# Gate and value products of a gated layer: eight block products per two-by-two block become Strassen's seven, in three chunks of 768 tokens

## The chip, the cores and the metric

The kernel runs on one core of one Trainium2 chip. The core has five engines with their own instruction streams, each worked off in order: PE (TensorE, matrix products into the eight PSUM banks), DVE (VectorE), ACT (ScalarE), POOL (GpSimd) and SP (SyncE, which here issues every DMA transfer). The metric is the time of one execution on the device, in microseconds (us). Lower is better.

## The reference

Three stages follow each other: attention with a decaying causal mask (4 batches, 8 heads, 576 positions, head size 64), a bilinear layer, and a gated layer with an RMS norm ahead of it. Cut to what matters:

```python
x = attention(q, k, v, f)                 # 2304 tokens x 512
x = ((x @ w1) * (x @ w2)) @ w3 @ w_out    # 512 -> 1024 -> 1024 -> 512
xn = x / sqrt(mean(x * x) + 1e-6) * g
gate, val = xn @ w_gate, xn @ w_val       # both 512 -> 1536
out = (silu(gate) * val) @ w_out2         # 1536 -> 512
```

## The kernel before

All data are 32-bit floats. PE multiplies them in its reduced format fp32r, and to keep the precision each operand is split into a high part (the value cast to fp32r) and a low part (the rest). One exact product is then three matmuls: high by high, high by low, low by high.

Nothing is issued in the order of the source. Every piece of work is entered in a planner (class `Plan`) with the engines that may do it, its assumed length, the names that it reads and writes and, for PE, a due time. `Plan.order` then writes out one static order for all engines. Work with two or three possible engines (`copy`, `sub`) goes to the one that would end it first.

The program has two parts in time. The first holds attention, the bilinear layer and the norm (lines up to 691); the normed tokens go to the DRAM tensor `yn_d`, transposed, 288 tokens at a time. The second is the gated layer, which the change rewrites:

- Tokens are taken in five chunks: four of 512 and one of 256. `load_x` fetches a chunk of `yn_d` and splits it into `xnh` and `xnl`, with two buffers, so that a chunk is ready long before it is needed.
- Over the 1536 hidden columns run 12 blocks `fb` of 128. For a block, `gv` makes two PSUM groups, gate and value, of 12 matmuls each (four pieces of the contraction by three passes, L762). They use two of the banks 0 to 3, and the next block uses the other two. ACT then takes the silu of the gate (L768), DVE multiplies it by the value (L769), ACT casts the result to `zh` (L770), and DVE subtracts for `zl` (L771).
- `wout` of the block before follows on PE: for each tile of 128 tokens three matmuls of 512 columns (L793) add into one of four accumulators (`wide`, banks 4 and 5). After the last block each accumulator is copied to one of two buffers `o` (L801 on DVE, L803 on ACT) and stored (L806).
- The weights come as 64-bit-wide data, 1 MB per block. `unit` loads a block into one of two buffers `raw`, converts it in place (Prelu on ACT, L553, and two integer operations on DVE, L554 and L555) and splits it into high and low tiles (L243 to L245, L236). In this kernel all 18 blocks of the second part are converted once, at 480 to 602 us, and stay in SBUF.

Of the kernel before, what the change touches and what calls it, by code (L numbers as in the profile page):

```python
# [13 lines left out]
F32 = mybir.dt.float32  # L14
# [8 lines left out]
P = 128  # L23
# [6 lines left out]
KF2 = DF2 // P  # L30
CH = S // 2
NEG = -1.0e30
FROWS = D + 4
# [5 lines left out]
PRE = 3  # L39
# [32 lines left out]
class Plan:  # L72
# [36 lines left out]
    def begins(self):  # L109

        ops = self.ops
        last = max(o[3] for o in ops if o[3] is not None) + 20000
        by = [last] * len(ops)
        for i in range(len(ops) - 1, -1, -1):
            alts, _, deps, at = ops[i]
            e, ns, _ = alts[0]
            t = by[i] - ns - self.LAG[e]
            if e == "SP":
                t -= 2250
            if at is not None and e == "PE":  # L120
# [81 lines left out]
def body(ctx, tc, q, k, v, f, w12, w3, wo1, wgv, wo2, g, out):  # L202
# [46 lines left out]
    def dma(nbytes, fn, r=(), w=(), at=0):  # L249
        plan.op([("SP", nbytes / (250 if nbytes < 2e5 else 420), False)], lambda e: fn(), r, w)  # L250
# [9 lines left out]
    cn_d = dram.tile([NH, 4, S], F32, name="cn_d")  # L260

# [6 lines left out]
    wpool = ctx.enter_context(tc.tile_pool(name="wpool", bufs=1))  # L268
    m1 = left.enter_context(tc.tile_pool(name="m1", bufs=1))
# [268 lines left out]
    def unit(raw, key, src, h_l, outkey, at, at_load, r_load=(), w_load=(), r_out=(), over=None, parts=1):  # L538

        r_out = list(r_out)  # L540
# [9 lines left out]

        act(1024, lambda: A.activation(f32(hi()), f32(hi()), AF.Prelu, scale=2.0**-112, alpha=2.0**32), [key], [kh], at, 210)  # L553
        dve(1024, lambda: V.tensor_scalar(out=lo(), in0=lo(), scalar1=2.0**-29, scalar2=7.0, op0=ALU.mult, op1=ALU.min), [key], [kl], at, rate=0.52, lock=True)  # L554
        dve(1024, lambda: V.scalar_tensor_tensor(out=lo(), in0=hi(), scalar=3, in1=lo(), op0=ALU.logical_shift_left, op1=ALU.bitwise_or), [key, kh], [kl], at, lock=True)  # L555
        n = 1024 // parts
        for c in range(parts):
            cs = slice(c * n, (c + 1) * n)
            ko = outkey + (c,) if outkey == ("w3",) else outkey
            wh, wl = ([ko + (m,)] + ([over + (m,)] if over else []) for m in "hl")  # L560
            copy(n, lambda cs=cs: h_l()[0][:, cs], lambda cs=cs: f32(lo()[:, cs]), [key, kl] + r_out, wh)
            sub(n, lambda cs=cs: h_l()[1][:, cs], lambda cs=cs: f32(lo()[:, cs]), lambda cs=cs: f32(h_l()[0][:, cs]), [key, kl, ko + ("h",)], wl)

    w12t = [[get(("W", i, m), wpool, [P, 1024], F32R, tag=f"W{i}{m}", name=f"W{i}{m}") for m in "hl"] for i in range(KF)]
    wo1t = [[get(("wo", i, m), wpool, [P, 1024], F32R, tag=f"W{4 + i}{m}", name=f"wo{i}{m}") for m in "hl"] for i in range(4)]
# [128 lines left out]
    chunks = [(c, min(512, NT - c)) for c in range(0, NT, 512)]  # L694
# [8 lines left out]
    w2units = []  # L703
    for fb in range(KF2):
        w2units.append(("wg", fb))
        if fb % 2 == 0:
            w2units.append(("wo2", fb // 2))
    w2t = {}
    for i, (kind, n) in enumerate(w2units):
        for m in "hl":  # L710
            tag = f"W{i - PRE}{m}" if PRE <= i < PRE + KF else f"{kind}{m}{n}"
            where_ = rpool if i < PRE else wpool if i < PRE + KF else lpool
            w2t.setdefault((kind, n), []).append(get((kind, n, m), where_, [P, 1024], F32R, tag=tag, name=f"{kind}{m}{n}"))
    raw2 = [get(("raw2", i), rpool, [P, 2048], F32, name=f"raw2{i}") for i in range(2)]
    xn2 = [[get(("xn", p, m), lpool if p else rpool, [P, KD, 512], F32R, name=f"xn{m}{p}") for m in "hl"] for p in range(2)]
    s_ = get("s", rpool, [P, 512], F32, name="s")
    z_t = [[get(("z", p, m), rpool, [P, 512], F32R, name=f"z{m}{p}") for m in "hl"] for p in range(2)]
    o_t = [get(("o", i), lpool, [P, DM], F32, name=f"o{i}") for i in range(2)]
    raw2n = [0]

    def w2_unit(i, at):
        kind, n = w2units[i]
        p = raw2n[0] % 2
        raw2n[0] += 1
        unit(raw2[p], ("raw2", p), (wgv if kind == "wg" else wo2)[n], lambda: tuple(t() for t in w2t[kind, n]), (kind, n), at, at,
             ["right"], (), ["left"] if i >= PRE + KF else (), ("W", i - PRE) if PRE <= i < PRE + KF else None)

# [3 lines left out]
    def load_x(ci, at):  # L731
        c, n = chunks[ci]
        p, rp = ci % 2, raw2n[0] % 2
        raw2n[0] += 1
        key = ("raw2", rp)

        def r():
            return raw2[rp]().rearrange("p (k n) -> p k n", k=KD)[:, :, 0:n]

        dma(2048.0 * n, lambda: SP.dma_start(out=r(), in_=yn_d[:, :, c:c + n]), yn_keys(c, n) + ["right"], [key, key + ("lo",), key + ("hi",)], at)  # L740
        for t in range(2):
            ks = slice(2 * t, 2 * t + 2)
            extra = ["left"] if p else []
            act(2 * n, lambda ks=ks: A.copy(xn2[p][0]()[:, ks, 0:n], r()[:, ks]), [key] + extra, [("xnh", p, t)], at)
            dve(2 * n, lambda ks=ks: V.tensor_sub(xn2[p][1]()[:, ks, 0:n], r()[:, ks], f32(xn2[p][0]()[:, ks, 0:n])),
                [key, ("xnh", p, t)] + extra, [("xnl", p, t)], at, lock=True)

    gvn = [0]

    def gv(ci, fb):  # L750
        n, p = chunks[ci][1], ci % 2
        gvn[0] += 1
        zp = gvn[0] % 2
        b_ = [2 * zp, 2 * zp + 1]
        t = [bank[i][:, 0:n] for i in b_]
        for m in range(2):
            def run(m=m):
                wh, wl = (w2t["wg", fb][i]().rearrange("p (m k i) -> p m k i", m=2, k=KD) for i in range(2))
                xh_, xl_ = (xn2[p][i]() for i in range(2))
                for kt in range(KD):  # L760
                    for i, (a, x) in enumerate(((wh, xh_), (wh, xl_), (wl, xh_))):
                        T.matmul(t[m], a[:, m, kt, :], x[:, kt, 0:n], start=(kt == 0 and i == 0), stop=(kt == KD - 1 and i == 2))  # L762
            pe(n, run, [("wg", fb, "h"), ("wg", fb, "l"), "right"] + [(a, p, i) for a in ("xnh", "xnl") for i in range(2)],
               [("bank", b_[m])], clock[0], 12)
            tick(12 * (2 + 0.4475 * n))
        at = clock[0]
        zh, zl = z_t[zp]
        act(n, lambda: A.activation(s_()[:, 0:n], t[0], AF.Silu), [("bank", b_[0]), "right"], ["s"], at)  # L768
        dve(n, lambda: V.tensor_mul(s_()[:, 0:n], t[1], s_()[:, 0:n]), [("bank", b_[1])], ["s"], at)  # L769
# [120 lines left out]
    for n, (kind, i) in enumerate(units):  # L890
# [4 lines left out]
        if (kind, i) == ("wo", 3):  # L895
            wc_group(0, WC0, WCP)
# [104 lines left out]
```

## Time and profile before

| | |
|---|---|
| time of the kernel, median of three runs (lowest, highest) | 1012.09 us (1010.34, 1013.09) |
| span of the profiled execution, first to last instruction | 1007.6 us |
| what lies around the span, from the median | 4.5 us |
| PE busy | 990.0 us, 98% of the span |
| DVE, ACT, POOL busy | 57%, 45%, 15% |
| chain of work that ended last | PE 88%, DVE 6%, ACT 2%, DMA 2% |
| first product of the gated layer on PE | 552.31 us |

Of the profiled execution only the span is recorded, no device time of its own; the last line but three is the difference of the median and this span. A busy PE says little by itself, because the recorded matmuls overlap: the end of each lies some 165 ns behind the start of the next. What a matmul costs in a dense stream is read from the distance of their starts, which the chain's pieces give (so many matmuls in so many us).

### The profile page before, as it was taken

Reading aid. Unit: us, or ns where it says so; the run is one execution under the profiler, and the core shown is the slowest. Engines: PE = TensorE matmul, PEld = TensorE weight load, DVE = VectorE, ACT = ScalarE, POOL = GpSimd, SP = SyncE. Lnnn points to the kernel's source line nnn. Section 1 sums busy time; section 2 is a strip of 40 time slices with the busy share of each in tenths; the row PEclk is TensorE's granted clock in tenths of the full one; section 3 lists DMA queues with packets and bytes.
Section 4 is the critical chain, followed back from the end, with each engine's and each line's share of the span. In section 5 each row is a group of like instructions: output and inputs, shape, how many; then the busy total and the mean of one; then the engine's idle time right before and its main releaser. Section 6 shows DMA issues by size and latency. Waiting matters only on the chain.

```text
span 1007.6 us, 15378 instructions
## 1 busy us (share of the span) xinstructions
PE 990.0 (98%) x5880; PEld 880.3 (87%) x5880; DVE 573.8 (57%) x1232; ACT 458.0 (45%) x1012; POOL 153.2 (15%) x197
## 2 busy tenths in 40 slices
PE   7899999999999999999999999999999999999997
PEld 4687889999999999999999888888888888888896
DVE  7899998787878778692959881221122111211121
ACT  6888786666765667563543431211122112111121
POOL 3165233213221231302022100000000000000000
PEclk9999999999999999999999999999999999999999
DMA  8853542121121211002435542010001000100010
GB/s 261 244 196 133 211 141 67 38 62 46 50 61 45 68 51 57 26 25 84 150 126 192 190 168 83 22 42 1 1 1 43 0 1 1 42 1 1 11 32 22
DMA packets 28002, 75.42 MB, mean 75 GB/s; under 512 B 3612, under 2 KB 12316, under 8 KB 23000
## 3 DMA queue, kind: packets, MB, share of 16 engines
q1 hardware_dynamic: 27928, 74.44, 22.5%
q8 instruction: 46, 0.75, 0.3%
q14 instruction: 28, 0.23, 0.1%
HBM read 64.38 MB, written 10.03 MB: 74 GB/s over the span
## 4 chain that ended last, share of the span: by engine, by line
PE 88%; DVE 6%; ACT 2%; DMA 2%; issue 1%; SPq 0%; ACTq 0%; DVEq 0%
PE bank L762 30%; PE bank L638 20%; PE bank L661 10%; PE wide L793 8%; PE bank L793 7%; PE bank L468 4%; PE wide L508 4%; PE bank L394 1%; PE bank L395 1%; DVE PTl L475 1%; DMA tmp<-in_f 1%; PE wide L395 1%; PE wide L394 1%; DMA rk<-x 1%; PE wide L514 1%
## 5 line engine op out<-in xcount | busy, mean ns | idle before, releaser
L769 DVE TENSOR_TENSOR s<-bank,s 128x512 f32<-128x512 f32 (+1 forms) x60 | 38.3, 638 | 275.9 <-PE bank L762 275.9
L762 PE MATMUL bank<-xnl,wgh 128*128 128x512 f32 (+1 forms) x480 | 177.8, 370 | 0.0
L762 PE MATMUL bank<-xnh,wgh 128*128 128x512 f32 (+1 forms) x480 | 177.8, 370 | 0.0
L762 PE MATMUL bank<-xnh,wgl 128*128 128x512 f32 (+1 forms) x480 | 177.4, 369 | 0.0
L768 ACT ACTIVATE s<-bank 128x512 f32<-128x512 f32 (+1 forms) x60 | 33.3, 555 | 191.8 <-PE bank L762 190.4
L762 PEld LDWEIGHTS bank<-xnh,wgh 128*128 128x128 f32 x480 | 90.3, 188 | 16.9
L762 PEld LDWEIGHTS bank<-xnl,wgh 128*128 128x128 f32 x480 | 90.4, 188 | 16.3
L762 PEld LDWEIGHTS bank<-xnh,wgl 128*128 128x128 f32 x480 | 90.3, 188 | 16.0
L770 ACT CAST zh<-s 128x512 fp32r<-128x512 f32 (+1 forms) x60 | 34.7, 578 | 131.7 <-DVE s L769 131.7
L475 DVE TENSOR_TENSOR PTl<-bank,PTh 128x512 fp32r<-128x512 f32 (+3 forms) x116 | 65.2, 585 | 27.5 <-ACT PTh L474 27.3
L661 PE MATMUL bank<-uh,Wch 128*128 128x288 f32 x256 | 77.1, 301 | 0.0
L661 PE MATMUL bank<-ul,Wch 128*128 128x288 f32 x256 | 75.7, 296 | 0.0
L661 PE MATMUL bank<-uh,Wcl 128*128 128x288 f32 x256 | 75.5, 295 | 0.0
L474 ACT CAST PTh<-bank 128x512 fp32r<-128x512 f32 (+3 forms) x116 | 54.5, 505 | 26.4 <-PE bank L468 21.7
L771 DVE TENSOR_TENSOR zl<-s,zh 128x512 fp32r<-128x512 f32 (+1 forms) x60 | 38.3, 638 | 34.4 <-ACT zh L770 34.4
L661 PEld LDWEIGHTS bank<-ul,Wch 128*128 128x128 f32 x256 | 48.2, 188 | 0.1
L661 PEld LDWEIGHTS bank<-uh,Wcl 128*128 128x128 f32 x256 | 48.2, 188 | 0.0
L661 PEld LDWEIGHTS bank<-uh,Wch 128*128 128x128 f32 x256 | 48.2, 188 | 0.0
L793 PE MATMUL wide<-wo2h,zh 128*128 128x512 f32 x120 | 47.5, 396 | 0.7 <-ACT o L803 0.7
L793 PE MATMUL wide<-wo2h,zl 128*128 128x512 f32 x120 | 47.5, 396 | 0.0
L793 PE MATMUL wide<-wo2l,zh 128*128 128x512 f32 x120 | 47.4, 395 | 0.0
L508 PE MATMUL wide<-PTl,V 128*128 128x512 f32 (+4 forms) x145 | 44.1, 324 | 0.9 <-DVE PTl L475 0.9
(350 smaller groups left out, 2538.9 us busy)
## 6 DMA issues: line engine op xcount, KB each, us to landing
raw<-in_wgv SPq DMA_DIRECT2D x12, 1024.0 KB
rk<-in_k SPq DMA_DIRECT2D x62, 144.0 KB
raw<-in_wo SPq DMA_DIRECT2D x6, 1024.0 KB
rv<-in_v SPq DMA_DIRECT2D x32, 160.0 KB
nrm<-in_w SPq DMA_DIRECT2D x5, 1024.0 KB
rq<-in_q SPq DMA_DIRECT2D x32, 144.0 KB
yn_d<-nrm SPq DMA_DIRECT2D x8, 576.0 KB
raw<-yn_d SPq DMA_DIRECT2D x4, 1024.0 KB
```

What stands on the lines that cost most here:

```text
L468: T.transpose(o[:, c * P:(c + 1) * P], PB[p][i][:, kb * P:(kb + 1) * P], ident)
L474: act(n, lambda: A.copy(PTh[:, pt:pt + n], o[:, lo:lo + n]), [], [("PTh", pt), key], at, 55)
L475: dve(n, lambda: V.tensor_sub(PTl[:, pt:pt + n], o[:, lo:lo + n], f32(PTh[:, pt:pt + n])), [("PTh", pt)], [("PTl", pt), key], at)
L508: pe(w, lambda s_=s_, o=o, w=w, c=c, kb=kb, m=m, src=src: T.matmul(t[:, o:o + w], V2[p][:, kb, :], src[:, c:c + w], start=(s_ == 0 and m = ...
L638: T.matmul(o, a, x[:, kt, :], start=(kt == 0 and i == 0), stop=(kt == KD - 1 and i == 2))
L661: T.matmul(o, a[:, es], x[:, ft, :], start=(ft == 0 and i == 0), stop=(ft == KF - 1 and i == 2))
L762: T.matmul(t[m], a[:, m, kt, :], x[:, kt, 0:n], start=(kt == 0 and i == 0), stop=(kt == KD - 1 and i == 2))
L768: act(n, lambda: A.activation(s_()[:, 0:n], t[0], AF.Silu), [("bank", b_[0]), "right"], ["s"], at)
L769: dve(n, lambda: V.tensor_mul(s_()[:, 0:n], t[1], s_()[:, 0:n]), [("bank", b_[1])], ["s"], at)
L770: act(n, lambda: A.copy(zh()[:, 0:n], s_()[:, 0:n]), ["s"], [("zh", zp)], at)
L771: dve(n, lambda: V.tensor_sub(zl()[:, 0:n], s_()[:, 0:n], f32(zh()[:, 0:n])), ["s", ("zh", zp)], [("zl", zp)], at, lock=True)
L793: T.matmul(acc2[t], a[:, ts_], w, start=(fb == 0 and i == 0), stop=(fb == KF2 - 1 and i == 2))
```

## The change

The two-by-two block structure is: the two halves of the contraction (256 each) by the gate and the value columns of a block, and for the tokens two halves of 384. Eight block products give gate and value for both halves of the tokens; the changed kernel forms them from seven products, by Strassen's method in Winograd's form.

- **Operands of the tokens.** `load_x` loads 768 tokens, forms four sums or differences of 128 x 768 and splits seven operands `xop` (there is one set, rewritten at each of the two changes of chunk).
- **Operands of the weights.** `widen` converts a raw block as before, puts four combinations of 128 x 256 into the free halves of the buffer and stores all of it in a DRAM tensor, `sw_d` (for the output weights `wo_d`, without combinations). For six gate and value blocks and three output blocks this is done during the first part (`todo`), for the others when chunk 0 first needs them. `load_w` loads a block for each of the 36 units (three chunks by 12 blocks) and splits it into one of three buffers `swt`, seven operands wide; in the second and third chunk the load is from `sw_d`. The six tiles of output weights still stay in SBUF.
- **A unit.** `gate(u)` makes seven products of six matmuls with 384 columns (L843), in two banks alone, 0 and 1, in turn. Three products start a bank anew and four add onto what stands there; between them ACT copies a bank out (`c1`, `c2`, `c5`) or takes the silu, and DVE adds (`c1`, `c5`, `c2`). The six `wout` tiles of the units before stand between the products. The accumulators of `wout` are now six: `wide` and banks 2 to 5.

The core of the diff (of the removed code only the products):

```diff
-        for m in range(2):
-            def run(m=m):
-                wh, wl = (w2t["wg", fb][i]().rearrange("p (m k i) -> p m k i", m=2, k=KD) for i in range(2))
-                xh_, xl_ = (xn2[p][i]() for i in range(2))
-                for kt in range(KD):
-                    for i, (a, x) in enumerate(((wh, xh_), (wh, xl_), (wl, xh_))):
-                        T.matmul(t[m], a[:, m, kt, :], x[:, kt, 0:n], start=(kt == 0 and i == 0), stop=(kt == KD - 1 and i == 2))
...
+NOP, TH = 7, 384
+TC = 2 * TH
...
+    def widen(kind, i, raw, key, w_load=(), r_load=(), at=None):
...
+            combine(256, t(0), b(3), b(0), keys[:2], [kh, tk[0]])
+            combine(256, t(2), b(2), b(3), keys, [tk[2]])
+            combine(256, t(1), b(2), t(0), keys + [tk[0]], [tk[1]])
+            combine(256, t(3), b(1), t(1), keys + [tk[1]], [tk[3]])
+            keys += tk
+        dma(1.05e6, lambda: SP.dma_start(out=(sw_d if kind == "wg" else wo_d)[i], in_=raw()), keys, [("wd", kind, i)], due=at)
...
+        for n, (c, e, src) in enumerate(((0, 768, lambda: lo()[:, 0:768]), (768, 1792, hi))):
+            split(e - c, lambda c=c, e=e: w()[:, c:e], lambda c=c, e=e: w()[:, SW // 2 + c:SW // 2 + e], src, keys + ["wfree" if b < 2 else "left"], ("sw", b, n, "h"), ("sw", b, n, "l"))
...
+            for kt in range(2):
+                for i, (a, c) in enumerate(((0, 0), (0, 1), (1, 0))):
+                    T.matmul(o, w[:, a, j, kt], x[c][:, kt], start=start and kt == 0 and i == 0, stop=kt == 1 and i == 2, skip_group_check=not start)
...
+        product(u, 0, 0, al, True)
+        act(TH, lambda: A.copy(c1(), pa), [ka] + free, ["c1"])
+        wout(u - 2, 4)
+        product(u, 1, 1, be, True)
+        dve(TH, lambda: V.tensor_add(c1(), c1(), pb), [kb], ["c1"])
+        act(TH, lambda: A.activation(s1(), c1(), AF.Silu), ["c1"] + free, [("s", 0)])
+        wout(u - 2, 5)
+        product(u, 4, 4, al, False)
+        act(TH, lambda: A.copy(c2(), pa), [ka] + free, ["c2"])
+        wout(u - 1, 0)
+        product(u, 3, 3, be, True)
+        act(TH, lambda: A.copy(c5(), pb), [kb] + free, ["c5"])
+        wout(u - 1, 1)
+        product(u, 5, 5, al, False)
+        dve(TH, lambda: V.tensor_add(c5(), c5(), pa), [ka], ["c5"])
+        wout(u - 1, 2)
+        product(u, 2, 6, be, False)
+        dve(TH, lambda: V.tensor_add(c2(), c2(), pb), [kb], ["c2"])
+        mix(s1, s1, c2, ["c2"], [("s", 0)])
+        z_out(u % 2, 0, s1)
+        wout(u - 1, 3)
+        product(u, 6, 2, al, False)
+        act(TH, lambda: A.activation(s2(), pa, AF.Silu), [ka] + free, [("s", 1)])
+        mix(s2, s2, c5, ["c5"], [("s", 1)])
+        z_out(u % 2, 1, s2)
```

How the static order moves is shown at three places. The first is PE in the steady state. Before, this is the end of one value group (bank_60 is bank 1) and the start of the output products behind it; `wgh`, `wgl` are the weights' parts, `xnh`, `xnl` those of the tokens:

```order
L762 MATMUL bank_60<-xnh_6281,wgh_6284 128x512
L762 MATMUL bank_60<-xnl_6288,wgh_6284 128x512
L762 MATMUL bank_60<-xnh_6281,wgl_6285 128x512
L793 MATMUL wide<-wo2h_6208,zh_6000 128x512
L793 MATMUL wide<-wo2h_6208,zl_6010 128x512
L793 MATMUL wide<-wo2l_6209,zh_6000 128x512
```

After, this is one whole unit of the last chunk; bank_59 and bank_60 are banks 0 and 1, the weights lie in `lbig` or `wbig`, L869 are the output products (bank_61 to bank_64 and `wide` are their accumulators):

```order
L843 MATMUL bank_59<-xop,lbig 128x384 x6
L869 MATMUL bank_64<-lbig,wbig 128x512 x3
L843 MATMUL bank_60<-xop,lbig 128x384 x6
L843 MATMUL bank_59<-xop,lbig 128x384 x6
L869 MATMUL wide<-lbig,wbig 128x512 x6
L843 MATMUL bank_60<-xop,lbig 128x384 x6
L843 MATMUL bank_59<-xop,lbig 128x384 x6
L869 MATMUL bank_61<-lbig,wbig 128x512 x3
L843 MATMUL bank_60<-xop,lbig 128x384 x6
L869 MATMUL bank_62<-lbig,wbig 128x512 x3
L843 MATMUL bank_59<-xop,lbig 128x384 x6
L869 MATMUL bank_63<-lbig,wbig 128x512 x3
```

A bank that was left alone for a whole block is now used again after two or three rows.

The second place is DVE in the middle of a chunk. Before (here around a change of chunk, with the split of a new chunk's tokens, L745):

```order
L769 TENSOR_TENSOR s<-bank_60,s 128x512
L745 TENSOR_TENSOR xnl_5215<-raw_5152,xnh_5198 128x1024 x2
L771 TENSOR_TENSOR zl_6063<-s,zh_6043 128x512
L769 TENSOR_TENSOR s<-bank_62,s 128x512
L771 TENSOR_TENSOR zl_6010<-s,zh_6000 128x512
```

After, in the eighth unit of chunk 0, where the blocks not combined earlier are combined; `lraw` holds raw weights, `cs` the copies and the gated values. Three rows of the unit follow these (L243, L252 and L243 on `cs`, 128x384):

```order
L901 TENSOR_TENSOR cs<-cs,bank_59 128x384
L561 SCALAR_TENSOR_TENSOR lraw<-lraw 128x1024
L739 TENSOR_TENSOR lraw<-lraw 128x256 x4
L252 TENSOR_SCALAR wbig<-lraw 128x768
L911 TENSOR_TENSOR cs<-cs,bank_60 128x384
L243 TENSOR_TENSOR wbig<-lraw,wbig 128x768
L243 TENSOR_TENSOR wbig<-lraw,wbig 128x1024
L914 TENSOR_TENSOR cs<-cs,bank_59 128x384
L560 TENSOR_SCALAR lraw<-lraw 128x1024
L890 TENSOR_TENSOR cs<-cs 128x384
L561 SCALAR_TENSOR_TENSOR lraw<-lraw 128x1024
L890 TENSOR_TENSOR cs<-cs 128x384
```

Where DVE had two instructions per block, it now has 18 in such a unit; L901, L911 and L914 are the ones that free a bank.

The third place is SP at the first change of chunk. Before, the stores follow each other:

```order
L740 DMA raw_5152<-yn_d 128x4x256
L806 DMA out<-o_6559 128x512
L806 DMA out<-o_6582 128x512
L806 DMA out<-o_6559 128x512
L806 DMA out<-o_6582 128x512
```

After, loads of weights for the next chunk stand between them:

```order
L806 DMA xf<-yn_d 128x4x768
L882 DMA out<-cs 128x512
L788 DMA lraw<-sw_d 128x2048
L882 DMA out<-cs 128x512
L788 DMA lraw<-sw_d 128x2048
L882 DMA out<-cs 128x512 x2
L882 DMA out<-cs 64x512
L788 DMA lraw<-sw_d 128x2048
L882 DMA out<-cs 64x512
L882 DMA out<-cs 128x512
```

The buffers of the stored tiles are still two, and a chunk stores six tiles where it stored four.

## Rows read from the trace of the kernel before

**Rows 1.** The page: busy us and share of each engine, PE in 40 slices

```profile
PE 990.0 (98%) x5880; PEld 880.3 (87%) x5880; DVE 573.8 (57%) x1232; ACT 458.0 (45%) x1012; POOL 153.2 (15%) x197
PE   7899999999999999999999999999999999999997
```

**Rows 2.** Windows: stretch, its length, then busy us (instructions) of each engine

```profile
core 0: us, PE busy (x) PEld busy (x) DVE busy (x) ACT busy (x) POOL busy (x), PEclk, DMA share, GB/s
100.00:130.00 30.00, 27.61 (x150) 23.21 (x148) 29.58 (x61) 24.57 (x48) 9.44 (x11) 1.00 0.57 204
130.00:440.00 310.00, 310.00 (x2339) 305.38 (x2340) 248.44 (x633) 208.21 (x529) 81.14 (x96) 1.00 0.19 56
552.30:602.00 49.70, 49.70 (x218) 40.58 (x217) 43.39 (x59) 21.10 (x27) 4.35 (x3) 1.00 0.52 182
602.00:948.30 346.30, 346.30 (x1505) 282.49 (x1504) 70.00 (x98) 59.63 (x96) 0.00 (x0) 1.00 0.05 17
```

**Rows 3.** Waits of PE from 130 us to the end

```profile
PE wide L793 <- ACT o L803: 0.7, 1, 0.7
PE bank L638 <- DVE Wcl L609: 0.6, 1, 0.6
```

**Rows 4.** Chain that ended last: start us, us, what; a block of 512 tokens

```profile
699.58 5.47 PE bank L762 x24
705.05 1.40 PE wide L793 x6
706.45 1.40 PE bank L793 x6
```

**Rows 5.** Chain: a block of 256 tokens; bilinear layer, last products of 288 columns

```profile
979.29 2.82 PE bank L762 x24
...
520.32 19.20 PE bank L638 x144
539.51 12.80 PE bank L661 x96
```

**Rows 6.** Weight loads of one block's products (one tile's instructions, 529 to 552 us)

```profile
L638 PEld LDWEIGHTS bank<-xhl,W6h x16: 187/188/188, 532.8 to 535.8; 128*128 128x128 f32 x16
```

**Rows 7.** DVE by line and shape: busy us, mean ns of one, idle before

```profile
L769 DVE TENSOR_TENSOR s<-bank,s 128x512 f32<-128x512 f32 x48 | 33.2, 691 | 244.1 <-PE bank L762 244.1
L475 DVE TENSOR_TENSOR PTl<-bank,PTh 128x384 fp32r<-128x384 f32 x29 | 16.0, 551 | 4.9 <-ACT PTh L474 4.8
L236 DVE TENSOR_TENSOR wgl<-raw,wgh 128x1024 fp32r<-128x1024 f32 x12 | 15.0, 1250 | 0.6 <-ACT wgh L243 0.5
L554 DVE TENSOR_SCALAR raw<-raw 128x1024 uint32<-128x1024 uint32 x18 | 13.6, 754 | 3.2 <-DMA raw<-in_wo 2.9 <-DMA raw<-in_wgv 0.3
L555 DVE SCALAR_TENSOR_TENSOR raw<-raw 128x1024 uint32<-128x1024 uint32 x18 | 22.7, 1259 | 3.2 <-ACT raw L553 3.0
L771 DVE TENSOR_TENSOR zl<-s,zh 128x256 fp32r<-128x256 f32 x12 | 5.1, 425 | 6.5 <-ACT zh L770 6.5
```

**Rows 8.** ACT by line and shape, columns as in group 7

```profile
L474 ACT CAST PTh<-bank 128x384 fp32r<-128x384 f32 x29 | 13.9, 481 | 2.3 <-PE bank L468 2.2
L744 ACT CAST xnh<-raw 128x1024 fp32r<-128x1024 f32 x8 | 8.3, 1050 | 3.4 <-PE bank L762 2.2 <-DMA raw<-yn_d 1.2
```

**Rows 9.** Timeline of DVE, SP: start us, us; successive instructions; a load and its first reader

```profile
541.13 0.45 DVE L236 TENSOR_TENSOR ul<-u,uh 128x288 fp32r<-128x288 f32 x1
541.50 0.69 DVE L245 TENSOR_SCALAR wo2h<-raw 128x1024 fp32r<-128x1024 f32 x1
...
543.51 0.33 SPq L542 DMA_DIRECT2D raw<-in_wgv  x1
...
548.37 0.88 DVE L554 TENSOR_SCALAR raw<-raw 128x1024 uint32<-128x1024 uint32 x1 [0.34 <-DMA raw<-in_wgv]
```

**Rows 10.** Timeline of ACT: a stored tile and the next tile in its buffer

```profile
656.18 0.59 ACT L803 COPY o<-wide 128x512 f32<-128x512 f32 x1 [2.90 <-PE wide L793]
...
658.97 0.59 ACT L803 COPY o<-bank 128x512 f32<-128x512 f32 x1 [1.68 <-DMA out<-o]
```

**Rows 11.** Timeline of the end

```profile
1002.48 0.40 PE L793 MATMUL wide<-wo2l,zh 128*128 128x512 f32 x1
1002.96 0.69 DVE L801 COPY o<-wide 128x512 f32<-128x512 f32 x1 [2.51 <-PE wide L793]
```

More of the change, by code (lines that the diff above doesn't have):

```diff
@@ L119, in begins @@
                 t -= 2250
-            if at is not None and e == "PE":
+            if at is not None:
                 t = min(t, at)
@@ L701, in lpool @@
         return pools2["l"]
[L703 to L726, printed above, removed]
+    def part(tile_, o, n):
+        return lambda: (tile_() if callable(tile_) else tile_)[:, o:o + n]
@@ new lines, in early, with load_w @@
+    def early(kind, i):
+        return i < (EARLY if kind == "wg" else (EARLY + 1) // 2)
+    loads = [0]
+    def load_w(kind, u):
+        n = loads[0]
+        loads[0] += 1
+        first = n < 3
+        raw, key = raw2[n % 2 + 2 * (not first)], ("raw3", int(first), n % 2)
+        i = u % KF2
+        r, w = ["right" if first else "left"], [("xr", j) for j in range(4)] + [("S", j) for j in range(3)] if first else []
+        if u < KF2 and not early(kind, i):
+            keys = widen(kind, i, raw, key, w, r)
+        else:
+            keys = [key, key + ("lo",), key + ("hi",)] + [key + ("t", j) for j in range(4)]
+            dma(1.05e6, lambda: SP.dma_start(out=raw(), in_=(sw_d if kind == "wg" else wo_d)[i]), [("wd", kind, i)] + r, keys + w)
+        lo, hi = lo_hi(raw)
+        if kind == "wo":
+            w = wot[i]
+            split(1024, lambda: w()[:, 0:1024], lambda: w()[:, 1024:2048], lo, keys + ["left" if i else "wfree"], ("wo2", i, "h"), ("wo2", i, "l"))
+            return
+        b = u % 3
+        w = swt[b]
+        for n, (c, e, src) in enumerate(((0, 768, lambda: lo()[:, 0:768]), (768, 1792, hi))):
+            split(e - c, lambda c=c, e=e: w()[:, c:e], lambda c=c, e=e: w()[:, SW // 2 + c:SW // 2 + e], src, keys + ["wfree" if b < 2 else "left"], ("sw", b, n, "h"), ("sw", b, n, "l"))
@@ L728, in yn_keys @@
     def yn_keys(c, n):
         return [("yn", i // 2, i % 2) for i in range(c // CH, (c + n - 1) // CH + 1)]
[L731 to L746, printed above, removed]
@@ L777, in rows @@
+    acc2 = [wide[:, 0:512], wide[:, 512:]] + bank[2:]
+    acc_keys = [("acc", 0), ("acc", 1)] + [("bank", i) for i in range(2, 6)]
     def rows(p0, n):
@@ new lines, in wout, with run @@
+    def wout(u, t):
+        if u < 0:
+            return
+        ch, fb = divmod(u, KF2)
+        zp = u % 2
+        ts_ = slice(t * P, (t + 1) * P)
+        def run():
+            w = wot[fb // 2]().rearrange("p (m t n) -> p m t n", m=2, t=2)[:, :, fb % 2]
+            zh, zl = (z_t[zp][m]() for m in range(2))
+            for i, (a, c) in enumerate(((zh, 0), (zl, 0), (zh, 1))):
+                T.matmul(acc2[t], a[:, ts_], w[:, c], start=(fb == 0 and i == 0), stop=(fb == KF2 - 1 and i == 2))
+        pe(512, run, [("wo2", fb // 2, "h"), ("wo2", fb // 2, "l"), ("z", zp, t // 3, "h"), ("z", zp, t // 3, "l")], [acc_keys[t]] + ["wide"] * (u == 0 and t < 2), clock[0], 3)
+        tick(3 * 231)
+        if fb == KF2 - 1:
+            o = o_t[t % 2]
+            r = ["wfree"]
+            if t % 2:
+                dve(512, lambda: V.tensor_copy(o(), acc2[t]), r, [acc_keys[t], ("o", t % 2)])
+            else:
+                act(512, lambda: A.copy(o(), acc2[t]), r, [acc_keys[t], ("o", t % 2)])
+            r0 = 0
+            for w_, tok in rows(ch * TC + t * P, P):
+                dma(262e3, lambda r0=r0, w_=w_, tok=tok: SP.dma_start(out=out[tok:tok + w_, :], in_=o()[r0:r0 + w_]), [("o", t % 2)])
+                r0 += w_
```

212 lines of the change are left out of this document (132 added, 80 removed).

## The prediction

> **What bounds the kernel now.** I read the page first: PE is busy 98% of the span, and its 40 slices are full from about 30 us to the last [rows 1]. Since recorded matmuls overlap, that alone proves little, so the second view is the waits of PE: behind 130 us PE waits twice, 0.7 and 0.6 us [rows 3]. The third is the windows. In the attention part (130 to 440 us) PE is covered while DVE works 248.4 of 310 us; at 552 to 602 us DVE works 43.4 of 49.7 us and PE still has no gap; from 602 us on DVE works 70 of 346 us. Only at 100 to 130 us does DVE fill its time (29.58 of 30), and there PE loses 2.4 us [rows 2]. So in the gated layer the time is the sum of PE's matmuls, and what shortens that sum shortens the kernel, until another engine or a wait takes over.
>
> The price of a matmul is the distance of starts in the chain. A block of 512 tokens, 24 products and 12 output products, takes 5.47 + 1.40 + 1.40 = 8.27 us; other blocks come to 8.31 and 8.35. I take 8.30, or 230.5 ns per matmul of 512 columns [rows 4]. One of 256 columns costs 2.82/24 = 117.5 ns, one of 288 19.20/144 = 133.3 ns [rows 5].
>
> **The change part by part.**
>
> *The products.* Before: 4 chunks x 12 blocks x 24 = 1152 matmuls of 512 columns and 288 of 256, so 1152 x 0.2305 + 288 x 0.1175 = 299.3 us. After: 36 units x 7 x 6 = 1512 matmuls of 384 columns, a width that the trace doesn't have. Between 256 and 512 columns the line gives 174.0 ns, between 288 and 512 it gives 175.0; I take 174.5, 263.8 us in all. Bounds: at the rate per column of 512 172.9 ns (261.4 us), at that of 288 177.7 ns (268.7 us). The weight load of 188 ns is longer than such a matmul, but the bilinear products load as long a weight every 133 ns [rows 5, 6], so loads overlap each other and add nothing. The output products stay: 648 of 512 columns. **Gain 35.5 us**, with bounds 30.6 and 37.9.
>
> The Trainium skill, "TensorE: Matmul & The Clock Gate", section "Back-to-back issue gap", gives for an isolated matmul N/2.4 + 2.5 ns: 215.8 at 512 columns, where this trace has 230.5. By it the products would go from 280.1 to 245.7 us, an estimate of 34.4 us of gain; the measured rows decide.
>
> *Bank reuse.* This is the new wait. Two banks serve seven products, so each next product in a bank waits until ACT or DVE has read it. By the order of PE, the narrow reuses have one output tile and one product between them: 0.70 + 6 x 0.1745 = 1.75 us. The wide ones have two tiles and one product, 2.44 us. The reader needs about 0.2 us until the last matmul has ended, then 481 ns on ACT or 551 ns on DVE for 384 columns [rows 7, 8]: 0.7 to 0.75 us. The narrow reuses (`c1`, `c5`) are ACT's, and ACT can have one operation of 1.05 us [rows 8] in front of them; DVE has only wide ones and can have one of 1.26 us [rows 7] and 0.4 us more. I cost the steady state at nothing; the cover is the output tiles between the products. Where DVE is crowded it costs something:
>
> *DVE in the first chunk.* The unit shown in the order has 7 instructions of 384 columns (551), 2 of L561 (priced as L555, 1259), 4 combinations of 256 (425), subtractions of 768 (970, between 512 and 1024) and 1024 (1250), L560 (754) and two copies (850 together, at the rate of 754 per 1024) [rows 7]: 11.9 us for 18 instructions. Successive ones start about 0.08 us before the last one's recorded end (541.13 + 0.45 against 541.50) [rows 9], so 10.5 us. PE needs 42 x 0.1745 + 18 x 0.2335 = 11.5 us for the unit. By the same sum over the order, units 1 to 13 lie between 8.5 and 11.6 us, 10.3 in the mean; later units need 5.9. DVE stays under PE, but by so little that some frees of a bank come late. The nearest rows go both ways: no loss at 87% of DVE's time, 2.4 us lost in 30 at 99% [rows 2]. I take 0.5 us in each of eight crowded units, **4 us lost**, bounds 0 and 10. POOL gets few instructions there, so its use of SBUF adds little.
>
> *Combining early.* Nine blocks in the first part add to DVE 9 x (0.75 + 1.26) us and nine combinations, some 21 us, and to ACT nine Prelu operations, against 62 us in which DVE is idle there [rows 2]. PE's order there changes only by a few swapped groups. **1 us lost**, bounds 0 and 3. DMA stores and loads go beside it; a 1 MB load takes 4.9 us from issue to first reader [rows 9], one per 11.5 us later, two buffers deep.
>
> *Start of the gated layer.* The first weights can only be split once the last bilinear products have freed their tiles. Behind these stand 12.8 us of output products of that layer [rows 5]; the splits of two blocks on DVE take some 6 us and a reload 4.9 us. Hidden; 0.5 us for the first unit, which has no output tiles between its products and a reuse of 1.05 us instead of 1.75.
>
> *Changes of chunk.* The one set of seven operands is rewritten during the last unit, each 11.5 us before its next use, with 7 x 0.97 us of subtractions. Six tiles are stored through two buffers: a buffer comes round in 2.79 us without other transfers [rows 10] while PE gives it 3.5 us; but SP now puts 1 MB loads between the stores, and a copy that waits for its buffer blocks ACT or DVE, and behind it a bank. I take **2 us at each of two changes**, bounds 0 and 4 each.
>
> *The end.* Before, the last copy starts 0.1 us after the last matmul, and 3.95 us lie from its end to the end of the span [rows 11]. After, six tiles end 0.70 us apart and go through two buffers of 2.79 us a round: with the first tile at 0, the sixth copy starts at 0.8 + 2 x 2.79 = 6.4, ends at 7.1, and the span at 11.0. The last matmul ends at 3.5, so 7.5 us remain instead of 4.7: **3 us lost**, bounds 1 and 5.
>
> *Sum.* 1007.6 - 35.5 + 4 + 1 + 0.5 + 4 + 3 = 984.6 us of span. With the 4.5 us by which the median of 1012.09 exceeds the span: 989.1, and I say 988.5.
>
> **The rivals.**
>
> *All of it hidden.* Nothing but the end is lost: 1007.6 - 35.5 + 3 + 4.5 = 979.6 us. For it speaks that PE has no gap at 87% of DVE's time, and that the order leaves each reuse 1 us or more to spare. Against it, DVE has about 11 of 11.5 us for several units in a row.
>
> *DVE is the bound of the first chunk.* If its instructions take 20% more than their rows, units of 10.3 us become 12.4, the longest 13.9, and 13 units lose some 0.9 us each, 12 us instead of 4. With all else as in the sum that is 997 us, and with twice the early loss and the upper bounds at the changes 1002. For it: the 30 us before 130, where DVE is full and PE waits [rows 2]. Against: only units 1 to 13 are crowded.
>
> *Each unit waits: slower than before.* The mechanism is the narrow reuse on ACT: two operations of 1.05 us in a row in front of `c1` or `c5` make its release 0.2 + 2.1 + 0.5 = 2.8 us, against 1.75. If that happens once in each of 36 units, PE loses 1.05 us each, 38 us: 989 + 38 - 4 = 1023 us. The gain is gone at 23/36 = 0.65 us per unit. Against it: in chunks 1 and 2 ACT has some 4.3 us of work per unit by the order, and weight splits can stand behind the wide reuses.
>
> *A matmul of 384 columns isn't cheaper by its columns.* If each waited for its 188 ns of weight load, 1512 x 0.188 = 284.3 us, the gain is 15.0 and the time 1009 us: no change. At 198 ns the products alone would take what they take now. The products of 288 columns [rows 5, 6] speak strongly against it.
>
> **How the numbers follow.** My forecast, PE still the bound with a few us lost in the crowded units, at the changes and at the end, has 0.62, its own range 981 to 996. All hidden: 0.12. DVE the bound: 0.14. No gain per matmul: 0.04. Each unit waits: 0.08. The range from 978 to 1004 leaves out the last two cases and tails of the others, under 0.2. A measurement of this kernel tells some 0.3% (3 us) from no change. Faster by more than that: 0.62 + 0.12 + 0.14 = 0.88; within it 0.04; slower 0.08.
>
> **What would show it.** The products right: chain pieces of about 1.05 us for six matmuls of 384 columns, and a unit of 11.5 us in chunks 1 and 2. Bank reuse free: no wait of PE on ACT or DVE copies of banks 0 and 1 in the second and third chunk. Crowded DVE: some waits of PE on L901, L911, L914 or on the weight splits at 552 to 710 us, 4 us in all, DVE busy at 90% or more. Changes: PE waits near 690 and 830 us, ACT or DVE idle on stores. Start of the layer within 2 us of 552. The end: 7.5 us from the last matmul. I am wrong if the unit of the last chunk takes over 12 us, or if PE has waits in every unit; then bank reuse or weight supply has become the bound.

## The result, and the profile after

The changed kernel takes 981.44 us (median of four runs, 979.75 to 986.86) where the kernel before, run beside it, takes 1011.3. The ratio is 0.9722, with a 95% interval of 0.969 to 0.9754: faster, by 29.9 us. The forecast was 988.5 with a range of 978 to 1004. The profiled execution has a span of 978.6 us and took 980.36, so 1.8 us lie around the span.

First the page, which answers to [rows 1]: busy time and share, then PE and DVE in 40 slices.

```profile
PE 955.2 (98%) x5952; PEld 890.7 (91%) x5952; DVE 739.5 (76%) x1526; ACT 528.4 (54%) x1157; POOL 181.8 (19%) x224
PE   7999999999999999999999999999999999999996
DVE  7999999798998878676544599998855557755542
```

PE is still full from end to end; it has 72 instructions more than before and 35 us less of busy time. DVE went from 57% to 76% of the span, and its slices show where: the run of nines in the middle lies in the first chunk of the gated layer, which starts at 551.63 us and lasts to about 700. The windows give the same by stage, with the columns of [rows 2]:

```profile
551.80:602.00 50.20, 49.47 (x260) 45.29 (x260) 44.70 (x77) 25.47 (x41) 3.97 (x4) 1.00 0.62 224
602.00:700.00 98.00, 96.00 (x498) 87.84 (x498) 87.25 (x143) 38.51 (x63) 4.20 (x4) 1.00 0.62 218
700.00:830.00 130.00, 129.39 (x681) 120.57 (x680) 81.12 (x130) 51.49 (x96) 2.39 (x2) 1.00 0.30 106
830.00:970.60 140.60, 139.43 (x729) 129.32 (x727) 76.76 (x127) 47.12 (x90) 1.05 (x1) 1.00 0.24 83
```

Up to 700 us DVE works 89% of the time and PE has some gaps; behind that DVE has 55 to 62%, and PE's only gap until the end is one of 0.61 us. The waits of PE from 130 us on, as in [rows 3]:

```profile
PE bank L843 <- ACT cs L919: 2.4, 3, 1.6
PE bank L843 <- DVE cs L901: 0.4, 2, 0.2
PE bank L843 <- ACT cs L905: 0.3, 1, 0.3
PE wide L869 <- DVE wbig L243: 0.2, 1, 0.2
```

So the new waits exist, but they are 3.3 us in all; DVE (L901, L243) ends 0.6 us of them, ACT 2.7. What the products cost stands in the chain of work that ended last (start, length, what); this is one unit of the last chunk:

```profile
909.30 2.08 PE bank L843 x12
911.38 1.37 PE wide L869 x6
912.75 2.08 PE bank L843 x12
914.84 0.69 PE bank L869 x3
915.53 1.04 PE bank L843 x6
916.57 0.69 PE bank L869 x3
917.25 1.04 PE bank L843 x6
918.29 0.69 PE bank L869 x3
918.99 1.04 PE bank L843 x6
920.03 0.69 PE bank L869 x3
920.71 2.08 PE bank L843 x12
```

The unit lasts from 909.30 to 920.71, 11.41 us, piece upon piece with nothing between. Six matmuls of 384 columns take 1.04 us and twelve 2.08, so one takes 173.3 ns. The unit's other 4.13 us are for its 18 output matmuls, 229.4 ns each.

Two gaps make most of the 2.4 us of L919. The timeline of ACT (start, length, line, instruction, in brackets the idle time before it and what ended it) shows what ACT stood at, and that of PE what followed:

```profile
667.02 0.89 ACT L250 ACTIVATE wbig<-lraw 128x768 fp32r<-128x768 f32 x1 [3.18 <-DMA lraw<-sw_d]
667.81 0.48 ACT L919 ACTIVATE cs<-bank 128x384 f32<-128x384 f32 x1
...
701.85 0.59 ACT L879 COPY cs<-bank 128x512 f32<-128x512 f32 x1 [5.99 <-DMA out<-cs]
702.33 0.50 ACT L919 ACTIVATE cs<-bank 128x384 f32<-128x384 f32 x1
```

```profile
668.34 1.32 PE L843 MATMUL bank<-xop,wbig 128*128 128x384 f32 x6 [1.57 <-ACT cs L919]
...
702.88 1.31 PE L843 MATMUL bank<-xop,wbig 128*128 128x384 f32 x6 [0.61 <-ACT cs L919]
```

In both, the instruction that PE needs (L919 reads a product's bank) is short and ready, but stands on ACT behind one that waits for a transfer: a split that waits for a reload of weights, and a copy of an output tile that waits for its buffer. The other two waits on ACT are of the same kind: ahead of 578.01 (0.3 us) ACT waited 1.71 us for a reload, ahead of 607.70 (0.18 us) 4.97 us for a load of raw weights.

The end, again by the chain, answers to [rows 11]:

```profile
966.75 0.60 ACT cs L879
...
967.37 0.70 DVE cs L877
...
968.61 2.36 DMA out<-cs
...
971.08 0.70 DVE cs L877
...
971.80 2.01 DMA out<-cs
...
973.94 0.69 DVE cs L877
```

DVE copies three tiles through one buffer, and each copy waits for the store of the one before it. The last matmul ends at 969.43; from there 9.2 us are left to the end of the span, where it was 4.7 before.

### The profile page after: what moved, and what is told of

It reads as the page before. It is cut to its first block, busy times and chain, and to the rows that moved or that the text cites. A ratio compares the mean times of both kernels' runs of the same rounds, so it can differ in the third digit from the quotient of the medians.

```text
span 978.6 us, 16159 instructions
## 1 busy us (share of the span) xinstructions
PE 955.2 (98%) x5952; PEld 890.7 (91%) x5952; DVE 739.5 (76%) x1526; ACT 528.4 (54%) x1157; POOL 181.8 (19%) x224
## 4 chain that ended last, share of the span: by engine, by line
PE 74%; DVE 14%; DMA 8%; issue 1%; ACT 1%; SPq 0%; DVEq 0%; ACTq 0%
PE bank L653 20%; PE bank L843 18%; PE bank L676 10%; PE bank L869 7%; PE bank L478 4%; PE wide L518 4%; PE wide L869 4%; PE bank L620 2%; DMA lraw<-in_wgv 2%; DVE wbig L243 2%; DMA xf<-yn_d 1%; PE bank L405 1%; PE bank L404 1%; DMA lraw<-sw_d 1%; DMA sw_d<-lraw 1%
## 5 line engine op out<-in xcount | busy, mean ns | idle before, releaser
L843 PE MATMUL bank<-xop,wbig 128*128 128x384 f32 x1008 | 194.4, 337 | 2.4 <-ACT cs L919 2.2
L843 PEld LDWEIGHTS bank<-xop,wbig 128*128 128x128 f32 x1008 | 177.7, 188 | 13.6 <-ACT cs L919 2.9
L653 PE MATMUL bank<-xhl,wbig 128*128 128x288 f32 x1152 | 169.4, 298 | 1.8 <-DVE xhl L243 1.2
L653 PEld LDWEIGHTS bank<-xhl,wbig 128*128 128x128 f32 x1152 | 157.1, 188 | 3.6 <-DVE xhl L243 1.8
L869 PE MATMUL bank<-lbig,wbig 128*128 128x512 f32 x360 | 100.1, 392 | 0.0
L843 PE MATMUL bank<-xop,lbig 128*128 128x384 f32 x504 | 98.3, 337 | 0.7 <-ACT cs L905 0.3
L843 PEld LDWEIGHTS bank<-xop,lbig 128*128 128x128 f32 x504 | 88.9, 188 | 7.2 <-DVE cs L901 0.7
L911 DVE TENSOR_TENSOR cs<-cs,bank 128x384 f32<-128x384 f32 x36 | 19.9, 552 | 82.4 <-PE bank L843 82.3
L869 PEld LDWEIGHTS bank<-lbig,wbig 128*128 128x128 f32 x360 | 66.2, 188 | 6.4
L653 PE MATMUL bank<-xhl,w 128*128 128x288 f32 x384 | 55.2, 296 | 0.0
L653 PEld LDWEIGHTS bank<-xhl,w 128*128 128x128 f32 x384 | 52.2, 188 | 0.0
L869 PE MATMUL wide<-lbig,wbig 128*128 128x512 f32 x180 | 47.9, 392 | 0.0
L243 DVE TENSOR_TENSOR wbig<-lraw,wbig 128x768 fp32r<-128x768 f32 (+1 forms) x44 | 47.5, 1090 | 0.4 <-ACT wbig L250 0.3
```

The lines of the kernel that those rows point to most:

```text
L243: plan.op([t_dve(n, lock=True), t_pool(n)], lambda e: on[e].tensor_sub(*(x() if callable(x) else x for x in (o, a, b_))), r, w)
L653: T.matmul(o, a, x[:, kt, :], start=(kt == 0 and i == 0), stop=(kt == KD - 1 and i == 2))
L843: T.matmul(o, w[:, a, j, kt], x[c][:, kt], start=start and kt == 0 and i == 0, stop=kt == 1 and i == 2, skip_group_check=not start)
L869: T.matmul(acc2[t], a[:, ts_], w[:, c], start=(fb == 0 and i == 0), stop=(fb == KF2 - 1 and i == 2))
L911: dve(TH, lambda: V.tensor_add(c5(), c5(), pa), [ka], ["c5"])
```

## The experiments

The theory is that of the prediction: the time of the gated layer is the sum of PE's matmuls, the reuse of the two banks is covered where DVE and ACT are free, and what is lost lies in the crowded first chunk and at the end. Rivals: the gain depends on something else than the number of products (reload traffic, the spacing of the banks), or the loss sits in every unit.

The start of the second part moves by some us from one execution to the next (last section). So besides the medians I compare one stretch of the profiled executions: from the first product of the gated layer (L843) to the end of the span. It is 427.0 us in the changed kernel (551.63 to 978.6). Each run has one profiled execution.

**An eighth product.** The first product of each unit is made twice.

```diff
         product(u, 0, 0, al, True)
+        product(u, 0, 0, al, True)
```

> Each unit makes its first product twice (the second overwrites the first, so nothing else changes): eight products of six matmuls as before the change, in the new frame of chunks, banks and reloads. Theory (PE's sum of matmuls is the time, a product costs 6 x 173.3 ns): 36 x 1.04 = 37.4 us more than the changed kernel's 981.4, less up to 3 us of waits that the longer units take up, so 1015 to 1019 us, 4 to 8 us over the kernel before; the frame alone then costs that much and the whole gain is the missing product. Rival (banks, DVE or weight supply set the pace of a unit, and PE has room): less than 25 us more, under 1006 us. A unit of chunk 2 takes 12.45 us by the theory.

Measured: 1015.34 us (1012.99 to 1018.83), ratio to the kernel before 1.0047 (1.0026 to 1.0068). A unit of the last chunk in its chain:

```profile
910.21 3.12 PE bank L843 x18
...
922.66 3.12 PE bank L843 x18
```

It is 12.45 us from one to the next, 1.04 more than in the changed kernel, just the six matmuls. With eight products the rebuilt kernel is no faster than the old one; the number of products is what the change gains by, and each of the seven is worth 36 x 1.04 = 37.4 us. The median grew by 33.9 and the stretch by 33.0: counted from start to start, the layer loses 2.0 us instead of 6.4 (how this is counted stands in the next section), and PE's recorded waits fell from 3.3 to 1.3 us. A longer unit leaves transfers, ACT and DVE more time; that this is why is argued, not tested.

**No reload in the third chunk.** Its 12 loads of 1 MB and their splits are left out.

```diff
-        if u < units2:
+        if u < 2 * KF2:
```

> The third chunk neither loads nor splits weights (it leaves out 12 loads of 1 MB and their splits, and computes that chunk with the weights that are left in the buffers). Theory (the reload lies wholly beside PE's matmuls, which need no slots in common with it): unit of the last chunk stays at 11.4 us, the time within 1.5 us of the changed kernel, 980 to 983 us. Rival (loads and splits take SBUF bandwidth or engine time from PE or from the frees of the banks): the unit gets shorter, at 0.3 us a unit 4 us less, 977 us or below.

Measured: 982.4 us (981.92 to 984.56). The unit in the chain:

```profile
900.34 2.08 PE bank L843 x12
...
911.75 1.39 PE bank L843 x8
```

11.41 us, the same to the hundredth, while ACT's work between 830 and 960 us falls from 45.46 to 30.32 us and the transfers from 85 to 13 GB/s. Weight reloading in the third chunk costs PE nothing. The stretch from the first product is 428.7 us, 1.7 more than in the changed kernel, and all of that is in waits ahead of 711 us, long before the third chunk: so much do the waits of the first chunk and its end vary from one execution to another.

**Combining none or all blocks early.** The number of the twelve gate and value blocks that are combined in the first part is 6 in the change; the output blocks move in proportion.

```diff
-EARLY = 6
+EARLY = 0
```

> No block is combined in the first part; all 18 are converted in chunk 0. By the order and the rows' durations DVE then has 10.8 to 14.1 us (150 us over 13 units) against 11.4 us of PE per unit. Theory (crowded DVE makes PE wait): 6 to 15 us more, 987 to 996 us, with the waits on bank frees and weight splits in chunk 0. Rival (DVE's crowding costs nothing, the waits seen are single late transfers): within 3 us of 981.4.

> All 18 blocks are converted, combined and stored in the first part instead of nine. Theory (the waits of PE in chunk 0 come from crowded DVE and the chains of loads and stores of converted blocks; the first part has DVE time to spare): waits between 552 and 720 us fall from 5.8 to about 2 us, the first product stays within 1 us of 551.6, so 977 to 979.5 us. Rival (the first part has no room left: 20 us more of DVE there delay it): first product 3 us or more later, 981 to 988.

Measured: with none 994.43 us (993.12 to 996.45), with all 981.37 (977.26 to 982.24). The windows of 602 to 700 us, first with none, then with all:

```profile
602.00:700.00 98.00, 90.92 (x456) 81.05 (x455) 88.06 (x154) 41.64 (x67) 2.22 (x2) 0.98 0.71 251
```

```profile
602.00:700.00 98.00, 98.00 (x517) 91.57 (x516) 66.72 (x107) 37.22 (x67) 1.00 (x1) 1.00 0.34 120
```

From the first product on they take 437.7 and 423.7 us, against 427.0 with six. So what is left to the first chunk costs the changed kernel some 3.3 us, and would have cost 14 had everything been combined there. DVE's own work is only a part of the reason. With none early DVE works 98% of the time up to 602 us and ends all of PE's waits there, 2.0 us. Behind that it is no busier than in the changed kernel (88.06 against 87.25 us), yet PE has 7.1 us of gaps instead of 2.0. Of its 9.7 us of waits in the layer 6.1 stand on ACT, and the four longest of these, 5.6 us, are reads of a bank that stand behind a conversion (L559) that waited for a load of raw weights. The longest:

```profile
659.40 1.15 ACT L559 ACTIVATE lraw<-lraw 128x1024 f32<-128x1024 f32 x1 [4.15 <-DMA lraw<-in_wgv]
660.46 0.46 ACT L905 COPY cs<-bank 128x384 f32<-128x384 f32 x1
```

That load is issued late, because the block that was combined in its buffer must first be stored. The waits of the DMA queue from 552 to 700 us show this (in all, times, longest; 24.5 us more stand on the stores of output weights):

```profile
SPq L550 <- DMA sw_d<-lraw: 39.9, 7, 8.2
```

The changed kernel has 17.0 and 14.0 us of the same waits; with all blocks early there is neither such a load nor such a wait. So the loss is one of the round through two raw buffers (load, convert, combine, store) at least as much as one of a busy DVE; no run tells the two apart, as a third buffer would. Behind the wait of 2.2 us at 660.97 the granted clock, too, is at 0.74 for 5 us, which costs an estimated (1 - 0.74) x 5 = 1.3 us.

The median of the version with all early shows nothing of the 3.3 us. Its profiled execution starts the layer 5.0 us later than the changed kernel's (556.66 against 551.63; see the last section); a later pair shows the gain.

**Output tiles behind the products.** All seven products of a unit follow each other and the six output tiles stand behind them. A bank then comes round after one product, 1.04 us, instead of 1.73 or 2.4.

```diff
         act(TH, lambda: A.copy(c1(), pa), [ka] + free, ["c1"])
-        wout(u - 2, 4)
         product(u, 1, 1, be, True)
...
         mix(s2, s2, c5, ["c5"], [("s", 1)])
         z_out(u % 2, 1, s2)
+        for t in range(6):
+            wout(u - 1, t)
```

PE's order of products and output tiles was also fixed to this one.

> All seven products of a unit follow each other, and the six output tiles stand behind the seventh; a bank that is used again after one product leaves its reader one product, 1.04 us, where it had 1.73 or 2.4. Theory (the output tiles between the products are cover against readers that come late, needed only where DVE or ACT is crowded): a free reader needs some 0.75 us, so the units of the second and third chunk wait a few tenths of a us at most; the units of the first chunk, where a split of 1 us or more can stand in front, lose most of the rest: 3 to 10 us in all, 984 to 992 us, steady unit of the last chunk 11.4 to 11.6 us. Rival (the spacing by output tiles is what carries the change in every unit): each unit waits 1 us or more, 36 us in all, 1017 us or more, and the waits stand on the copies and sums of banks 0 and 1 in all three chunks.

Measured: 1004.07 us (1002.11 to 1007.04), ratio to before 0.9944. That is 22.6 us above the change and outside both forecasts, between them. Which of the two theories is nearer, the unit of the last chunk tells:

```profile
909.41 7.28 PE bank L843 x42
916.69 1.37 PE wide L869 x6
918.07 2.72 PE bank L869 x12
920.79 7.28 PE bank L843 x42
```

11.38 us, with 42 matmuls of 384 columns in 7.28 us: no wait at all, although each bank comes round after one product. The rival, that every unit waits, is out. The loss is in the first chunk and at the first change of chunk, and it is larger than expected. PE's gaps sum to 17.6 us between 545 and 830 us, against 3.3. Sixteen of its waits, 11.2 us, lie ahead of 700 us, most of them on a sum of DVE (L900 is here the sum that was L901):

```profile
PE bank L843 <- DVE cs L900: 5.8, 7, 1.3
```

So in the first chunk the shorter spacing does let DVE's lateness through, which in the changed kernel costs 0.6 us. The other two, on PE and then on DVE (L907 is the sum that was L911):

```profile
714.83 2.29 PE L843 MATMUL bank<-xop,wbig 128*128 128x384 f32 x6 [3.84 <-DVE cs L907]
...
730.40 1.36 PE L843 MATMUL bank<-xop,wbig 128*128 128x384 f32 x6 [2.50 <-DVE cs L907]
```

```profile
710.87 3.43 DVE L739 TENSOR_TENSOR xf<-xf 128x768 f32<-128x768 f32 x2 [3.33 <-DMA xf<-yn_d]
714.23 0.54 DVE L907 TENSOR_TENSOR cs<-cs,bank 128x384 f32<-128x384 f32 x1
...
729.20 0.69 DVE L877 COPY cs<-bank 128x512 f32<-128x512 f32 x1 [4.80 <-DMA out<-cs]
729.80 0.55 DVE L907 TENSOR_TENSOR cs<-cs,bank 128x384 f32<-128x384 f32 x1
```

DVE waited for the load of the next chunk's tokens, and then for the store of an output tile, and the short sum behind it was late. In the changed kernel the first sum that needs this load stands behind the two that free a bank; here the planner put it ahead of them. So this version changes more than the spacing, and how much of its loss is due to the spacing alone is not settled. It does show how a wait on DMA reaches PE. The clock then adds to it:

```profile
715.00:720.00 5.00, 5.00 (x18) 4.41 (x19) 3.11 (x6) 2.06 (x4) 0.00 (x0) 0.71 0.00 2
...
730.00:735.00 5.00, 4.59 (x15) 3.84 (x16) 4.93 (x9) 1.95 (x3) 0.00 (x0) 0.66 0.38 105
```

Behind each of the two gaps the granted clock, a mean over its two levels of 1.2 and 2.4 GHz, stands at 0.71 and 0.66 of the full one for 5 us, and then at 1.00 again: an estimated (0.29 + 0.34) x 5 = 3.2 us more. The products also began 2.4 us later in this execution: 66 of them stand ahead of the last bilinear matmul, which starts at 565.29, and 565.42 less 66 x 0.1733 is 553.98, against 551.63. The gaps as they are recorded are smaller than what they cost, since the end of a matmul's record lies behind the start that a next one could have had: the 36 products from 704.30 would let the next start at 710.54, it starts at 714.83, 4.29 us later where 3.84 are recorded. Counted from start to start, from 553.98 to 0.23 us behind the start of the last matmul at 992.74, this version loses 27.8 us in the layer, the clock included, 21.3 more than the changed kernel; with the 2.4 us of the start that is the 23.7 us by which the spans differ.

**Store buffers.** Output tiles go through four buffers instead of two.

```diff
-    o_t = [part(cs, 5 * TH + i * DM, DM) for i in range(2)]
+    o_t = [part(cs, 5 * TH + i * DM, DM) for i in range(4)]
```

> Four buffers for stored tiles instead of two. Theory (the 9.2 us from the last matmul to the end are six tiles going through two buffers): the last copy starts 0.1 us after the last matmul and the end is 4.7 to 5 us behind it, as in the kernel before; the wait of 0.8 us at the first change of chunk, where a copy waits for a store, goes too. 4 to 5 us less: 976 to 977.5 us. Rival (the landing of the stores, not the buffers, sets the end): no change, 980 to 982.

Measured: 979.86 us (979.24 to 983.7). The end comes 6.4 us behind the last matmul instead of 9.2, and the stretch from the first product is 424.0 instead of 427.0, so 3 us are there in the profile, where 4 to 5 were expected; of the median only 1.6 is seen, within what the runs scatter. The end misses the 4.7 to 5 us of the theory because the sixth copy still waits 2.36 us for the store of the second tile. PE has no wait at the change of chunk, as expected, but its waits in the first chunk are longer than in the changed kernel's execution.

**Both together.** Twelve early blocks, four buffers, and two more for the last chunk; then, on one chip, the same again beside its twin with six early blocks.

```diff
-EARLY = 6
+EARLY = 12
...
-            o = o_t[t % 2]
+            last = ch == NT // TC - 1
+            oi = t if last else t % 4
```

> Twelve blocks combined in the first part instead of six, four buffers for stored output tiles instead of two, and six in the last chunk. Theory (what the change loses lies in the crowded first chunk, where the early kernel had 3.3 us back, and at the end, where six tiles go through two buffers): from the first product to the end of the span 419 to 421 us instead of 427.0, the end 4.7 to 5.5 us behind the last matmul instead of 9.2, 974 to 978 us. Rival (the two don't add, since the early work costs the first part what the second gains): 979 to 982 us, with the first product 2 us or more later than 551.6 and the granted clock full.

> Six blocks combined early, as in the change, with the store buffers of the best version (four, and six in the last chunk). Theory (early combining of twelve blocks gives 3.3 us behind the first product and takes nothing ahead of it): 3 us longer than the best version's 978.0, 980 to 982 us; from the first product to the end of the span 423 to 424 us. Rival (twelve early blocks take from the first part what they give the second): 977 to 979 us, like the best version.

> The best version once more, beside the one with six early blocks. Theory: 976 to 979 us again, 2 to 4 us below the other; rival: the same as the other within 1 us.

Measured: 977.97 us (976.07 to 978.76), then 975.48 (973.92 to 976.58) with a ratio to before of 0.9647 (0.9623 to 0.9672), and with six early blocks 978.77 (977.16 to 983.92), 0.9689. The stretch from the first product is 420.0, 419.6 and 422.6 us. Here the 3.3 us of the early blocks are seen in the medians as well, and the ranges of the two versions don't overlap: the two gains add, and in this pair the first part does not pay for them. In the earlier pair, of the changed kernel and the version with all early, the medians were the same, so that a price of some us in the first part is not excluded. PE's waits in the layer in the fastest of them are three of 0.2 us. Its last copy:

```profile
967.88 0.69 DVE L879 COPY xf<-bank 128x512 f32<-128x512 f32 x1 [0.67 <-PE bank L869]
```

The last copy now waits for PE alone. The end is 5.9 us behind the last matmul, a little over the 4.7 to 5.5 expected; probably because the eight stores of six tiles are still issued one behind the other (965.77 to 970.61). This version is the fastest of all, 35.6 us below the kernel before.

## Why the prediction was right, step by step

- **PE's matmuls bound the gated layer: right.** The eighth product adds its own 1.04 us to each unit, and leaving out loads and splits takes nothing away.
- **The price of 384 columns: right, near the lower bound.** 174.5 ns was taken, 173.3 measured, so 1512 products take 262.1 instead of 263.8 us, 37.2 less than the 299.3 of before. The rival by which each matmul pays 188 ns of weight load is out. The Trainium skill, "TensorE: Matmul & The Clock Gate", section "Back-to-back issue gap", gives by its formula, N/2.4 + 2.5, an estimate of 162.5 ns for an isolated matmul of this width; the chain has 10.8 ns more, and at 512 columns before it had 14.7 more (230.5 against 215.8).
- **Bank reuse free where DVE and ACT are: right**, and with more to spare than claimed. I named the output tiles between the products as the cover; without them the unit of the last chunk still has no wait. The tiles are cover only where an engine is late, as in the first chunk.
- **Crowded DVE, 4 us: near in size, mostly wrong in cause.** Counted in starts, the layer takes 417.6 us from the first product (551.63) to where a next matmul could follow the last (969.04, its start, and 0.23). The matmuls' prices sum to 262.1 + 648 x 0.2294 = 410.7, and the norm's two matmuls take 0.5, so 6.4 us are lost in starts, where 4 + 0.5 + 4 had been forecast for crowd, start and changes. The change of chunk has 0.9 of them (at 702.88), which leaves 5.5 for start and crowd, where 4.5 had been forecast. The step that didn't hold is that DVE, with 11 of PE's 11.5 us, frees banks late: of the 3.3 us of recorded waits DVE ended 0.6, in waits of 0.2 us, and the largest, 1.57 us at 668.34, is ACT's, behind a split whose reload was late. Twelve early blocks remove that wait and give 3.3 us back in all. So the size came out partly by luck. DVE was busy 89% of the time there, where I had said 90 or more.
- **Changes of chunk, 2 us each: too much.** The first cost 0.9 us, in the way forecast (a copy behind its store); with four store buffers this wait is gone. The second cost nothing: behind the gap of 0.61 us at 702.88 the windows show no more of PE until its last matmul. The split at 667.02 is of the next chunk's first weights, but it stands some 30 us ahead of the change and with twelve early blocks, when no raw block goes through the same buffers, it is not late.
- **Combining early, 1 us: nothing seen.** The first product comes 0.5 us earlier than before, 551.63 against 552.15. (The 552.31 given for the kernel before is the chain's figure; the chain's pieces start 0.16 us behind the timeline's.) What twelve early blocks cost the first part is not settled, as said above.
- **The end: the mechanism right, too small.** 3 us were taken, within bounds of 1 and 5; it lost 4.4. Two figures of its working were off, by 0.8 us each: the sixth copy starts 7.2 us behind the first, not 6.4, and the last matmul ends 2.7 us behind the first copy's start, not 3.5. I gave each round of a buffer 2.79 us; the second took 2.86 (971.08 to 973.94), but the first 3.71 (967.37 to 971.08). And I counted five tiles behind the first copy; it waits for both tiles of `wide`, so that four stand behind it (966.75 to 969.43).
- **The sum.** The span came out at 978.6 instead of 984.6 us: 1.7 less from the products, 2.1 from the waits (6.4 instead of 8.5), 1.5 from the first part, 0.7 from the output matmuls (229.4 ns instead of the 230.5 of the kernel before), and 1.4 more at the end, 4.6 less in all. The other 1.4 us lie in the kernel before, whose layer took 450.6 us from the first product (552.15 to 1002.71), 1.9 more than the 448.7 of its matmuls in my sum; 0.5 of these are the norm's two matmuls, which both kernels have. I then added 4.5 us for what lies around the span. That was a difference between a median and one execution, and the measured value is 1.8; this put the forecast another 2.7 us too high.

So the case "all hidden", 979.6 us and a chance of 0.12, came nearer in its number than the forecast, but not in its reasons: the losses were there.

## What to carry to other kernels

Where PE is full, a product saved is worth its matmuls at the spacing of starts that the chain shows, also when the engines beside it take on more work (here 739.5 us of DVE instead of 573.8); the cost lies where that work and its transfers are crowded, and can be moved to where there is room. Look for short instructions that free a bank and stand behind one that waits for DMA: their lateness reaches PE, and the clock may drop on top of it. At the end of a kernel, store buffers are worth their space: four instead of two took 2.8 us off, six another 0.5.

## What the runs showed of the hardware

Between kernels whose first parts are nearly the same, the first product of the gated layer starts anywhere from 551.3 to 557.0 us. Part of it is the clock in the first 50 us, an estimated (1 - 0.83) x 10 = 1.7 us: the three executions that start it at 556.65 to 557.03 have a granted clock of 0.83 in one stretch of 10 us there, and so has one that starts it at 553.8; four of 551.3 to 554.5 and the changed kernel itself have 1.00. With twelve early blocks it starts at 554.1 to 557.0, with six at 551.3 to 554.5, which is too few executions to part the two. In the best version's first profile, one of the three, PE waits 3.1 us for a transfer (of `cn_d`) ahead of the drop (1.1 in the changed kernel); the stretches of 30 to 40 and 40 to 50 us:

```profile
30.00:40.00 10.00, 6.87 (x39) 4.89 (x38) 7.37 (x18) 5.27 (x14) 0.94 (x2) 1.00 0.97 265
40.00:50.00 10.00, 9.83 (x46) 7.38 (x45) 9.00 (x17) 9.71 (x21) 3.08 (x2) 0.83 0.41 144
```

Why that transfer takes longer in one execution than in another stays open. So does the small difference of the output matmuls, 229.4 ns against 233 before (1.40 us for six [rows 4]): no run was made for it.
